# One side pair in each of eight K/Q steps, K first, with a padded hT and kv constants set ahead of the fold

## The chip, the core and the metric

The kernel runs on one core of a Trainium2 chip. A core has five engines with queues of their own: TensorE (PE, matrix products), VectorE (DVE), ScalarE (ACT, activations), GpSimd (POOL) and SyncE (SP, which issues DMAs). They meet only at semaphores. TensorE writes into eight PSUM banks of 512 float32 columns. The metric is the device time of one execution in microseconds (us), lower is better; the number for a kernel is the median of several runs.

## What is computed

The input x (2048 tokens, 448 features) is normalised (LN1) to xn. Two branches read xn and are added to x: a linear attention whose feature map is a softmax of q or k times a learned w_phi and of its negative, and an MLP mixer with a GELU layer, token shifts of 1, -1, 2 and -2 on four feature groups, a second product (W2), a second layer norm (LN2) and an MLP with W3 and W4. Cut to what matters:

```python
def A(x, wqkv, w_phi, wo):                       # 16 heads of 28
    q, k, v = heads(x @ wqkv)
    phi_q = concat([softmax(q @ w_phi), softmax(-(q @ w_phi))])
    phi_k = concat([softmax(k @ w_phi), softmax(-(k @ w_phi))])
    kv, z = phi_k.T @ v, phi_k.sum(tokens)
    return ((phi_q @ kv) / (phi_q @ z + 1e-6)) @ wo

def B(x, w1, w2, w3, w4):
    h = gelu(layernorm(x) @ w1)                  # 448 wide
    hs = concat([shift(h[:, 112*m:112*m+112], s) for m, s in enumerate((1, -1, 2, -2))]) @ w2
    x1 = x + hs
    return x1 + gelu(layernorm(x1) @ w3) @ w4    # 1792 wide inside

xn = layernorm(x)
out = x + A(xn, wqkv, w_phi, wo) + B(xn, w1, w2, w3, w4)
```

## The kernel before

Tokens are 16 tiles of 128, or 4 groups of 512. The program is written as one list of operations (class Recorder): each is appended to the queue of its engine in the order of the code, and `solve` puts a semaphore wait ahead of an operation wherever it touches a piece of memory that another engine wrote or reads. Pieces are tracked by whole PSUM banks and, in SBUF, by grains of 32 bytes of a row (and by halves of 64 partitions). Two tensors or rows that share a grain are therefore ordered even if no byte is common. A queue runs strictly in its order, so a wait holds all that stands behind it.

hT holds the GELU outputs transposed, four feature groups m in a row of the region, each HW = S + 8 = 2056 columns of two bytes, 4112 bytes: 128 and a half grains.

The stages, in order: LN1, the transposes of xn, V of the first tiles and W1 (`octet`); the fold of w_phi into wq and wk (`phi_blocks` makes a block-diagonal matrix bd in the tile g_tok by a product with a mask on VectorE; `fold` multiplies by it; VectorE casts the results to wpk and wpq); then the K/Q steps; then W3 by pairs of 128 features (`w3_pair`, its two halves are a(p) and b(p) in the last list), attention outputs (`num_tile`, N) and the last product (`fin_pair`, f), all by the order written out in `play([...])`.

A K/Q step ps (0 to 7) handles two token tiles of K in banks 2 and 3 (`k_pair`), half a token group of Q in banks 0 and 1 (`q_pair`), and, where `side` names one, a W2 pair or a V pair of two tiles in banks 4 and 5. Each pair is two halves of matmuls, k[0] and k[1] and so on, because the 448 rows of a contraction are split over 64-row halves of the array that run two at a time. Then come: two exponentials of K and two of Q on ScalarE; the kv products of two tiles from two steps earlier, which accumulate in banks 6 and 7 (`kv_tile`); `w2_out`, four VectorE additions that take W2 out of its banks into xn; `k_norm`, a sum and a reciprocal for each tile on VectorE and a product on POOL (1697 ns a tile); `w2_norm`, the LN2 statistics on VectorE, and after each fourth tile the scale (`ln_scale`) on POOL; `g_apply`, the LN2 result of one tile in g_tok on POOL, which `g_T` later transposes by a DMA on SP's queue into gT, the input of W3. In step 6 `kv_picks` clears a matrix (pick, shown as tile w) on POOL and fills it by four copies on VectorE; `kv_copy` and `kv_blocks` use it after all kv products to bring kv into place.

`late_3` sets constants: the padding of wpq and phik, zeros in kvq on POOL, and then ones in a column of kvq for each of four heads on VectorE. In the code it stands ahead of the fold, so its operations do so in the queues too.

Of the kernel before, what the change touches and what calls it, by code (L numbers as in the profile page):

```python
# [223 lines left out]
def bass_parallel_sum__linear_kernel_hedgehog__mixer_s_mlp__prompt_kernel(  # L224
    nc, A_x, A_wqkv, A_w_phi, A_wo, B_x, B_w1, B_w2, B_w3, B_w4, out,
):
    _, S, D = A_x.shape
# [3 lines left out]
    NT, NG, KC, NC, NM, FC, HP = 16, 4, 4, 4, 4, 14, 32  # L231
    CR = 112
    SHIFTS = [1, -1, 2, -2]
    HW = S + 8
    x2d, out2d = A_x[0], out[0]

    es = ExitStack()
    with es:
        R = Recorder(nc, es)
        total = [0]  # L240

        def region(name, nbytes):
            nbytes = -(-nbytes // 64) * 64
            total[0] += nbytes
            h = es.enter_context(nc.sbuf_tensor(name, [128, nbytes // 2], BF16))
            R.track(h, nbytes)
            return h

        def view(h, cols, dt=BF16, at=0):
            a = h[:, at // 2:at // 2 + cols * DTB[dt] // 2]  # L250
            return a if dt == BF16 else a.bitcast(dt)

        def new(name, cols, dt=BF16):
            return view(region(name, cols * DTB[dt]), cols, dt)
# [12 lines left out]
        xnT = view(xnT_r, KC * S).rearrange("p (c s) -> p c s", c=KC)  # L267
        hT_r = region("hT", NM * HW * 2)
        hT = view(hT_r, NM * HW).rearrange("p (m s) -> p m s", m=NM)
        phik_r = region("phik", NT * 1024 * 2)  # L270
# [21 lines left out]
        kvq = new("kvq", 8 * 64).rearrange("p (b e) -> p b e", b=8)  # L292
# [48 lines left out]
        dve, pool = "DVE", "POOL"  # L341
# [59 lines left out]
             [maskb[0:CR, :]], [maskb[0:CR, :]])  # L401

        def late_3():
            R.ew(pool, "memset", wpq.rearrange("p c (h e) -> p (c h) e", e=HP)[:, :, DH:HP], 0.0)
            R.ew(pool, "memset", phik.rearrange("p t g e -> p (t g) e")[:, :, DH:HP], 0.0)
            R.ew(pool, "memset", kvq[:, :, :], 0.0)
            for h in range(4):
                col = HP * (h % 2) + DH + 1
                R.ew(dve, "memset", kvq[HP * h:HP * h + DH, :, col:col + 1], 1.0)
# [5 lines left out]
        def lap(a):  # L415
            return bass.AP(a.tensor, a.offset, [list(a.ap[0]), [192, 2], [1, 256]])

        def halves(a):
            return a.rearrange("p (b e) -> p b e", b=2)
# [12 lines left out]
        def ln_apply(eng, dst, src, mvt, rst, i):  # L432
            m, op = (mvt[:, i, 0:1], ALU.subtract) if eng == dve else (rst[:, i, 1:2], ALU.add)
            R.ew(eng, "tensor_scalar", dst, src, m, rst[:, i, 0:1], op0=op, op1=ALU.mult)
# [73 lines left out]
        def two(b):  # L508
            return pairs[b // 2].rearrange("p (b e) -> p b e", b=2)

        def w1_parts(g, bs):
            def evac():
                for m in (0, 2):
                    R.act(hT[0:CR, m:m + 2, 2 + 512 * g:2 + 512 * g + 512], two(bs[m])[0:CR, :, :], ACT.Gelu_apprx_tanh)
            return (lambda k: banks[bs[k]][0:CR, :],
                    lambda m, kc, lo, hi: w1[lo:hi, kc, CR * m:CR * m + CR],
                    lambda m, kc, lo, hi: xnT[lo:hi, kc, 512 * g:512 * g + 512]), evac
# [20 lines left out]
        def row_pairs(first, second, start=False):  # L538
            for s, (p, q) in enumerate(zip(first, second)):
                for out, lhs, rhs in (p, q):  # L540
                    R.mm(out, lhs, rhs, start and s == 0, False)

        def lap_pair(outs, lhs, rhs):
            def side(k, rows, kcs):
                return [(outs[k], lhs(k, kc, *rows), rhs(k, kc, *rows)) for kc in kcs]
            return (lambda: row_pairs(side(0, LO, (0, 1, 2, 3)), side(1, HI, (0, 1, 2, 3)), True),
                    lambda: row_pairs(side(1, LO, (0, 1, 3)), side(0, HI, (0, 2, 3))))
# [16 lines left out]
        def w2_pair(i, b):  # L564
            def side(k, lo, hi):
                r = []
                for m in range(NM):
                    c0 = 2 + 128 * (i + k) - SHIFTS[m]
                    r.append((banks[2 * b + k][:, 0:D], hT[lo:hi, m, c0:c0 + 128], w2[lo:hi, m, :]))
                return r  # L570
            return (lambda: row_pairs(side(0, 0, 64), side(1, 64, CR), True),
                    lambda: row_pairs(side(1, 0, 64), side(0, 64, CR)))

        def w2_out(i, b):
            for k in range(2):
                a = banks[2 * b + k]
                R.ew(dve, "tensor_tensor", xn[:, i + k, 0:256], a[:, 0:256], xn[:, i + k, 0:256], op=ALU.add)
                R.ew(dve, "tensor_tensor", xn[:, i + k, 256:D], a[:, 256:D], xn[:, i + k, 320:512], op=ALU.add)
# [52 lines left out]
        def g_apply(i):  # L631
            ln_apply(pool, halves(g_tok[:, i % 4, :]), lap(xn[:, i, :]), mv2, rs2, i)
# [44 lines left out]

        def w3_pair(p):
            g, fc = divmod(2 * p, FC)
            b = p % 2  # L680
            a = lap_pair([banks[2 * b + k] for k in range(2)],
                         lambda k, kc, lo, hi: w3[lo:hi, kc, 128 * (fc + k):128 * (fc + k) + 128],
                         lambda k, kc, lo, hi: gT[lo:hi, g % 2, kc, :])

            def late():
                a[1]()
                R.act(h3T[:, g % 2, fc:fc + 2, :], two(2 * b), ACT.Gelu_apprx_tanh)
            return a[0], late
# [70 lines left out]
        v, w = v_parts(0, (4, 5, 6, 7)), w1_parts(0, (0, 1, 2, 3))  # L759
# [7 lines left out]
        v, w = v_parts(8, (4, 5, 6, 7)), w1_parts(1, (0, 1, 2, 3))  # L767
        octet(w[0], ([], [(xn_T, 10, 4)], [(xn_T, 11, 5)]), w[1], v[0], ([], [(phi_blocks, 0)]), v[1])
        a, b = w1_parts(2, (0, 1, 2, 3)), w1_parts(3, (4, 5, 6, 7))
# [6 lines left out]
        def w2_norm(i):  # L776
            for j in (i, i + 1):
                ln_stats(st2, mv2, xn, j)
            if i % 4 == 2:
                ln_scale(mv2, rs2, i - 2, 4, 4)  # L780

        wa, wb = w2_pair(0, 1), w2_pair(2, 0)
        wa[0]()
        wb[0]()
        wa[1]()
        w2_out(0, 1)
        wb[1]()
        w2_out(2, 0)
        w2_norm(0)
        w2_norm(2)  # L790
        side = {1: ("w", 4), 2: ("w", 6), 3: ("v", 12), 4: ("v", 14), 5: ("w", 8), 6: ("w", 10)}
        for ps in range(8):
            k, q = k_pair(2 * ps, 1), q_pair(ps // 2, 2 * (ps % 2), 0)
            kind, i = side.get(ps, ("", 0))
            w = {"w": w2_pair, "v": v_pair}[kind](i, 2) if kind else ()
            k[0]()
            if w:
                w[0]()
            else:
                q[0]()  # L800
            k[1]()
            for s in range(2):
                k_exp(2 * ps, 1, s)
            if ps > 1:
                kv_tile(2 * ps - 4)
                kv_tile(2 * ps - 3)
            if w:
                q[0]()
                w[1]()
            if kind == "w":  # L810
                w2_out(i, 2)
            if kind == "v":
                R.act(vaug[:, i:i + 2, :].rearrange("p t (h e) -> p t h e", e=HP)[:, :, :, 0:DH],
                      two(4)[:, :, 0:D].rearrange("p t (h e) -> p t h e", e=DH), ACT.Copy)
            q[1]()
            for s in range(2):
                q_exp(2 * ps, 0, s)
            k_norm(2 * ps)
            if kind == "w":
                w2_norm(i)  # L820
            if ps > 0:
                g_apply(ps - 1)
            if ps == 4:
                for i in range(4):
                    g_T(i)
            if ps == 6:
                kv_picks()
# [3 lines left out]
        wl = {i: w2_pair(i, 2) for i in (12, 14)}  # L831

        def a(p):
            return (w3p[p][0],)

        def b(p):
            return (w3p[p][1],)
# [4 lines left out]
        def N(i):  # L842
            return (lambda: (num_tile(i), o_T(i)),)

        def K(*t):
            return (lambda: [kv_tile(i) for i in t],)

        def w2_last(i):
            wl[i][1]()
            w2_out(i, 2)  # L850
            w2_norm(i)

        def G(*t):
            return (lambda: [g_T(i) for i in t],)
# [4 lines left out]
        def A(*t):  # L859
            return (lambda: [g_apply(i) for i in t],)  # L860

        play([
            a(0), (wl[12][0],), b(0), a(1), (w2_last, 12), b(1), A(7), K(12, 13), G(4, 5),
            a(2), (wl[14][0],), b(2), a(3), (w2_last, 14), b(3), G(6, 7), A(8, 9, 10, 11),
            K(14, 15), (kv_copy,), a(4), a(5), b(4), (kv_blocks,), b(5),
            a(6), N(0), b(6), a(7), f(1, 0), b(7), N(1), a(8), b(8), f(2, 0), G(8, 9), a(9), N(2), b(9),
            a(10), f(3, 0), b(10), f(4, 0), G(10, 11),
            a(11), N(3), b(11), f(1, 1), a(12), N(4), b(12), f(2, 1), S(0, 1),
# [49 lines left out]
```

## Time and profile before

| | us |
|---|---|
| three runs | 190.83, 192.46, 193.15 |
| median | 192.46 |
| profiled execution, time on the device | 190.65 |
| its span, first to last instruction | 188.9 |

A row of the timeline reads: start, length, engine, line of the code, operation, written tile, read tiles, shape, how many were merged, and in brackets how long the engine had been idle just before and what ended that. Lines L203, L207, L211 and L215 are the helpers that record every operation, so the tiles tell what a row is: bank<-wpk,xnT is K, bank<-xnT,wpq is Q, bank<-w,hT is W2, bank<-gT,w is W3, bank<-vaug,phik is kv, bank<-xnT,w with 112 rows is W1. On VectorE, xn<-bank,xn is the taking out of W2, ksum the norms of K, st the LN2 statistics (of xn). On ScalarE, phik<-bank of 896 elements are the exponentials of K, eq_lo and hi those of Q. Matmuls are pipelined: the length of a group runs past the start of the next, so the pace is read from start to start.

### The profile page before, as it was taken

The numbers are of one execution on the slowest core, as the hardware profiler recorded it, in microseconds if no ns is written. First come the engines' busy times: TensorE is split into PE (matmuls) and PEld (weight loads), VectorE is DVE, ScalarE is ACT, GpSimd is POOL, SyncE is SP. The second block draws the span as 40 slices with busy tenths as digits, with TensorE's granted clock in tenths as the row PEclk, the third lists the DMA queues.
The fourth block names the chain that finished last, engine by engine and source line by source line (L and its number), as shares of the span: only waits on it lengthen the run. The fifth ranks groups of instructions, "written<-read, shape, count | busy, mean of one in ns | idle before, by whom it ended". The sixth has DMA issues, their size and how long they took to land.

```text
span 188.9 us, 4746 instructions
## 1 busy us (share of the span) xinstructions
PE 174.6 (92%) x2031; PEld 97.6 (52%) x2031; DVE 113.0 (60%) x282; ACT 82.4 (44%) x92; POOL 97.2 (51%) x144
## 2 busy tenths in 40 slices
PE   7699979987999997589899999999999999999993
PEld 5345535433669975245554555454555545555451
DVE  5799636388799669666864375154642536464531
ACT  2359833708869977654463242222422224224000
POOL 5667850005679998848275226844062440732740
PEclk9999999999999999999999999999999999999999
DMA  5994259930001111110201243203532030211321
GB/s 169 371 223 87 54 100 371 348 94 0 3 9 24 28 31 28 31 28 4 55 5 28 59 70 73 76 0 80 111 59 76 3 88 20 76 31 28 79 78 48
DMA packets 32979, 14.85 MB, mean 79 GB/s; under 512 B 24703, under 2 KB 32447, under 8 KB 32959
## 3 DMA queue, kind: packets, MB, share of 16 engines
q1 hardware_dynamic: 31710, 13.58, 28.9%
q10 hardware_dynamic: 1248, 0.98, 1.6%
q8 instruction: 16, 0.26, 0.6%
q14 instruction: 5, 0.03, 0.1%
HBM read 7.08 MB, written 1.84 MB: 47 GB/s over the span
## 4 chain that ended last, share of the span: by engine, by line
PE 72%; DVE 12%; POOL 7%; ACT 4%; issue 2%; DVEq 0%
PE bank L203 72%; DVE xn L215 4%; DVE st L215 3%; POOL rs L215 3%; ACT hi L211 2%; ACT phik L211 2%; POOL xn L215 2%; DVE mv L215 1%; DVE ksum L215 1%; POOL phik L215 1%; POOL mv L215 1%; DVE vaug L215 1%; DVE w L215 1%; ACT hT L211 1%; DVE rks L215 0%
## 5 line engine op out<-in xcount | busy, mean ns | idle before, releaser
L211 ACT ACTIVATE phik<-bank 128x1024 bf16<-128x1024 f32 (+1 forms) x44 | 42.3, 984 | 70.0 <-PE bank L203 70.0
L203 PE MATMUL bank<-gT,w 64*128 64x512 bf16 x392 | 50.6, 377 | 2.6 <-ACT hi L211 2.5
L215 DVE TENSOR_TENSOR vaug<-bank,vaug 128x464 f32<-128x464 f32 (+3 forms) x65 | 32.6, 512 | 25.1 <-PE bank L203 23.5
L203 PE MATMUL bank<-w,phik 64*128 64x448 bf16 (+1 forms) x420 | 45.0, 349 | 0.1
L215 POOL TENSOR_TENSOR xnT<-vaug 128x196 bf16<-128x196 f32 (+1 forms) x32 | 18.1, 585 | 45.9 <-DVE vaug L215 45.9
L203 PEld LDWEIGHTS bank<-w,phik 64*128 64x128 bf16 (+1 forms) x420 | 21.7, 94 | 21.8 <-PE bank L203 0.5
L215 POOL TENSOR_TENSOR phik<-phik,rks 128x896 bf16<-128x896 bf16 x16 | 26.8, 1697 | 7.3 <-DVE rks L215 7.3
L203 PEld LDWEIGHTS bank<-gT,w 64*128 64x128 bf16 x392 | 18.6, 94 | 20.2 <-ACT hi L211 3.0
L215 DVE TENSOR_REDUCE ksum<-phik 128x32 f32<-128x896 bf16 x16 | 16.8, 1052 | 1.7 <-ACT phik L211 1.7
L203 PE MATMUL bank<-xnT,wpq 64*128 64x512 bf16 x112 | 16.3, 376 | 1.5 <-ACT hi L211 1.3
L215 POOL TENSOR_SCALAR mv<-mv 128x1 f32<-128x1 f32 (+2 forms) x16 | 3.6, 225 | 26.6 <-DVE mv L215 26.0
L215 DVE RECIPROCAL vaug<-bank 128x16 f32<-128x16 f32 x16 | 4.1, 257 | 21.8 <-PE bank L203 21.8
L215 POOL TENSOR_TENSOR vaug<-xn,xtok 128x448 f32<-128x448 bf16 x16 | 16.2, 1031 | 1.2 <-DVE vaug L215 1.2
L203 PE MATMUL bank<-wpk,xnT 64*128 64x448 bf16 x112 | 15.0, 349 | 1.4 <-ACT phik L211 1.2
L203 PE MATMUL bank<-w,hT 64*128 64x448 bf16 (+1 forms) x128 | 15.6, 350 | 0.4 <-ACT hT L211 0.4
L203 PE MATMUL bank<-xnT,w 128*112 128x512 bf16 (+1 forms) x64 | 14.7, 385 | 1.4 <-DVE g_tok L215 1.4
L215 DVE TENSOR_TENSOR xn<-bank,xn 128x256 bf16<-128x256 f32 (+1 forms) x32 | 10.0, 378 | 8.6 <-PE bank L203 8.6
L203 PE MATMUL bank<-wv,xnT 64*128 64x448 bf16 (+1 forms) x76 | 13.6, 352 | 0.3 <-DVE xn L215 0.2
L203 PE MATMUL bank<-wo,xnT 64*128 64x448 bf16 (+1 forms) x106 | 13.4, 349 | 0.0
L215 POOL TENSOR_SCALAR g_tok<-xn,rs 128x512 bf16<-128x512 bf16 x16 | 12.1, 767 | 0.0
L215 POOL TENSOR_TENSOR rs<-mv,mhalf 128x1 f32<-128x1 f32 (+2 forms) x16 | 11.3, 705 | 1.3
L211 ACT ACTIVATE hT<-bank 112x1024 bf16<-112x1024 f32 x8 | 7.9, 1024 | 7.7 <-PE bank L203 7.7
(67 smaller groups left out, 182.9 us busy)
## 6 DMA issues: line engine op xcount, KB each, us to landing
w<-in_B_w_dram SPq DMA_DIRECT2D x2, 896.0 KB, 5.8
out_dram<-vaug SPq DMA_DIRECT2D x15, 112.0 KB, 1.9
w<-in_B_w_dram SPq DMA_DIRECT2D x1, 1568.0 KB, 11.8
xtok<-in_A_x_dram SPq DMA_DIRECT2D x2, 448.0 KB, 6.8
xtok<-in_A_x_dram SPq DMA_DIRECT2D x2, 224.0 KB, 5.1
w<-in_B_w_dram ACTq DMA_DIRECT2D x2, 224.0 KB, 5.3
wo<-in_A_wo_dram SPq DMA_DIRECT2D x2, 224.0 KB, 6.9
w<-in_B_w_dram SPq DMA_DIRECT2D x1, 392.0 KB, 8.0
```

What stands on the lines that cost most here:

```text
L203: self.op("PE", lambda e: e.matmul(out, lhsT, rhs, start=start, stop=stop, skip_group_check=True), [out], [lhsT, rhs], tile=self._tile(lhsT))
L211: self.op("ACT", lambda e: e.activation(out, in_, func, **kw), [out], [in_] + aps)
L215: self.op(eng, lambda e: getattr(e, name)(out, *args, **kw), [out], aps)
```

## The change

Five edits. The rows of hT are padded from 2056 to 2064 columns (4128 bytes, 129 whole grains). `late_3` clears kvq first, and the ones in kvq leave it for a function `kv_ones`, called after the fold. The two W2 pairs ahead of the K/Q steps move into steps 0 and 1, and the list `side` gives each of the eight steps one W2 or V pair, so that each step runs k[0], w[0], k[1], kv, q[0], w[1], q[1]. `g_apply` runs two steps behind instead of one, and the first four `g_T` move from step 4 to step 5. The W3 pairs swap banks (the first one in 2 and 3), and the statistics of the last two W2 pairs move later in the list.

```diff
-    HW = S + 8
+    HW = S + 16
...
         def late_3():
+            R.ew(pool, "memset", kvq[:, :, :], 0.0)
             R.ew(pool, "memset", wpq.rearrange("p c (h e) -> p (c h) e", e=HP)[:, :, DH:HP], 0.0)
             R.ew(pool, "memset", phik.rearrange("p t g e -> p (t g) e")[:, :, DH:HP], 0.0)
-            R.ew(pool, "memset", kvq[:, :, :], 0.0)
+
+        def kv_ones():
             for h in range(4):
...
         def w3_pair(p):
             g, fc = divmod(2 * p, FC)
-            b = p % 2
+            b = 1 - p % 2
...
-        wa, wb = w2_pair(0, 1), w2_pair(2, 0)
-        wa[0]()
-        wb[0]()
-        wa[1]()
-        w2_out(0, 1)
-        wb[1]()
-        w2_out(2, 0)
-        w2_norm(0)
-        w2_norm(2)
-        side = {1: ("w", 4), 2: ("w", 6), 3: ("v", 12), 4: ("v", 14), 5: ("w", 8), 6: ("w", 10)}
+        kv_ones()
+        side = [("w", 0), ("w", 2), ("w", 4), ("v", 12), ("v", 14), ("w", 6), ("w", 8), ("w", 10)]
...
             k[0]()
-            if w:
-                w[0]()
-            else:
-                q[0]()
+            w[0]()
             k[1]()
...
-            if w:
-                q[0]()
-                w[1]()
+            q[0]()
+            w[1]()
...
-            if ps > 0:
-                g_apply(ps - 1)
-            if ps == 4:
+            if ps > 1:
+                g_apply(ps - 2)
+            if ps == 5:
                 for i in range(4):
                     g_T(i)
...
         def w2_last(i):
             wl[i][1]()
             w2_out(i, 2)
-            w2_norm(i)
...
-            a(0), (wl[12][0],), b(0), a(1), (w2_last, 12), b(1), A(7), K(12, 13), G(4, 5),
+            a(0), (wl[12][0],), b(0), a(1), (w2_last, 12), b(1), (w2_norm, 12), A(6, 7), K(12, 13), G(4, 5),
             a(2), (wl[14][0],), b(2), a(3), (w2_last, 14), b(3), G(6, 7), A(8, 9, 10, 11),
-            K(14, 15), (kv_copy,), a(4), a(5), b(4), (kv_blocks,), b(5),
+            K(14, 15), (kv_copy,), (w2_norm, 14), a(4), a(5), b(4), (kv_blocks,), b(5),
```

On POOL, ahead of the fold, the memset of kvq moves past those of wpq and phik:

```order
 L215 TENSOR_SCALAR xn<-xtok,rs 128x512
+L215 MEMSET kvq 128x512
 L215 MEMSET wpq 128x64x4
 L215 MEMSET phik 128x512x4
-L215 MEMSET kvq 128x512
```

It is first of the three now; the four VectorE memsets that read its result stand behind all casts of the fold.

On TensorE, from the last W1 matmuls to the second K/Q step:

```order
 L203 MATMUL bank<-g_tok,hi 128x112 x4
 L203 MATMUL bank<-xnT,w 112x512 x6
-L203 MATMUL bank<-w,hT 128x448 x32
 L203 MATMUL bank<-wpk,xnT 128x448 x8
+L203 MATMUL bank<-w,hT 128x448 x8
+L203 MATMUL bank<-wpk,xnT 128x448 x6
 L203 MATMUL bank<-xnT,wpq 128x512 x8
-L203 MATMUL bank<-wpk,xnT 128x448 x6
+L203 MATMUL bank<-w,hT 128x448 x8
 L203 MATMUL bank<-xnT,wpq 128x512 x6
 L203 MATMUL bank<-wpk,xnT 128x448 x8
```

The block of 32 W2 matmuls is gone from there; its first half stands in step 0 between the halves of K and of Q, its second half in step 1.

On VectorE, at the end of step 6 and in step 7, before:

```order
L215 BN_STATS st<-xn 128x6
L215 BN_AGGR mv<-st 128x2
L215 COPY w<-ident 32x128 x4
L215 TENSOR_REDUCE ksum<-phik 128x32
L215 RECIPROCAL rks<-ksum 128x32
```

and after:

```order
L215 BN_STATS st<-xn 128x6
L215 BN_AGGR mv<-st 128x2
L215 COPY w<-ident 32x128 x4
L215 TENSOR_TENSOR xn<-bank,xn 128x256
L215 TENSOR_TENSOR xn<-bank,xn 128x192
L215 TENSOR_TENSOR xn<-bank,xn 128x256
L215 TENSOR_TENSOR xn<-bank,xn 128x192
L215 TENSOR_REDUCE ksum<-phik 128x32
L215 RECIPROCAL rks<-ksum 128x32
```

Step 7 has a W2 pair now, and its `w2_out` stands right behind the copies that fill pick, which wait for POOL. What POOL does ahead of that memset (w), before:

```order
L215 TENSOR_TENSOR phik<-phik,rks 128x32x28 x2
L215 TENSOR_SCALAR mv<-mv 128x4
L215 TENSOR_TENSOR rs<-mv,mhalf 128x4
L215 TENSOR_SCALAR rs<-mv 128x4
L215 TENSOR_SCALAR g_tok<-xn,rs 128x512
L215 MEMSET w 128x256
```

and after:

```order
L215 TENSOR_TENSOR phik<-phik,rks 128x32x28 x2
L215 TENSOR_SCALAR g_tok<-xn,rs 128x512
L215 MEMSET w 128x256
L215 TENSOR_TENSOR phik<-phik,rks 128x32x28 x2
L215 TENSOR_SCALAR mv<-mv 128x4
L215 TENSOR_TENSOR rs<-mv,mhalf 128x4
```

The scale of four tiles that stood ahead of the memset comes a step later, behind the K norms of step 7.

More of the change, by code (lines that the diff above doesn't have):

```diff
@@ L780, in w2_norm @@
                 ln_scale(mv2, rs2, i - 2, 4, 4)
-        wa, wb = w2_pair(0, 1), w2_pair(2, 0)
-        wa[0]()
-        wb[0]()
-        wa[1]()
-        w2_out(0, 1)
-        wb[1]()
-        w2_out(2, 0)
-        w2_norm(0)
-        w2_norm(2)
-        side = {1: ("w", 4), 2: ("w", 6), 3: ("v", 12), 4: ("v", 14), 5: ("w", 8), 6: ("w", 10)}
+        kv_ones()
+        side = [("w", 0), ("w", 2), ("w", 4), ("v", 12), ("v", 14), ("w", 6), ("w", 8), ("w", 10)]
         for ps in range(8):
             k, q = k_pair(2 * ps, 1), q_pair(ps // 2, 2 * (ps % 2), 0)
-            kind, i = side.get(ps, ("", 0))
-            w = {"w": w2_pair, "v": v_pair}[kind](i, 2) if kind else ()
+            kind, i = side[ps]
+            w = {"w": w2_pair, "v": v_pair}[kind](i, 2)
             k[0]()
-            if w:
-                w[0]()
-            else:
-                q[0]()
+            w[0]()
             k[1]()
```

## Prediction, made before the changed kernel was run

> **What bounds the kernel now.** I read the page's first part, then TensorE's list of waits, then the timeline of each engine from 24 us to 95 us, then the windows by stage.
>
> ```profile
> PE 174.6 (92%) x2031; PEld 97.6 (52%) x2031; DVE 113.0 (60%) x282; ACT 82.4 (44%) x92; POOL 97.2 (51%) x144
> PE bank L203 <- ACT hi L211: 3.8, 2, 2.5
> 44.47:80.77 36.30, 32.26 (x480) 24.29 (x480) 28.99 (x60) 28.93 (x33) 30.83 (x26) 1.00 0.10 20
> ```
>
> TensorE is the bound, and the change removes none of its matmuls, so all it can win is TensorE's idle time, all of which that can move lies before 95 us. In the third row (one window: length, busy time of PE, PEld, DVE, ACT, POOL, then granted clock, DMA share, GB/s) TensorE idles 4.0 us in the K/Q steps, most of it in the two waits of the second row.
>
> The first place is the fold of w_phi, in the timeline:
>
> ```profile
> 24.22 0.39 PE L203 MATMUL bank<-g_tok,rsel 28*112 28x448 bf16 x1
> 25.48 0.52 POOL L215 MEMSET kvq<- 128x512 bf16 x1
> 26.09 0.46 DVE L215 MEMSET kvq<- 28x8 bf16 x4 [3.24 <-POOL kvq L215]
> 26.56 0.62 DVE L215 TENSOR_TENSOR g_tok<-bank,maskb 112x448 bf16<-112x448 f32 x1
> 27.24 0.85 PE L203 MATMUL bank<-xnT,w 128*112 128x512 bf16 x3 [1.39 <-DVE g_tok L215]
> ```
>
> The mask product (26.56) could have run once its matmul ended at 24.61. Four small memsets stood ahead of it in VectorE's queue and waited for POOL's memset of kvq, third of three. TensorE waited 1.39 us.
>
> The second place is the opening of W2 and the first K/Q step:
>
> ```profile
> 35.41 0.74 PE L203 MATMUL bank<-w,hT 64*128 64x448 bf16 x6
> 36.60 2.63 PE L203 MATMUL bank<-w,hT 64*128 64x448 bf16 x26 [0.44 <-ACT hT L211]
> 36.56 1.28 ACT L211 ACT_TABLE_LOAD   x1
> 39.26 0.36 PE L203 MATMUL bank<-wpk,xnT 64*128 64x448 bf16 x1
> 44.47 0.93 PE L203 MATMUL bank<-wpk,xnT 64*128 64x448 bf16 x8 [1.17 <-ACT phik L211]
> ```
>
> W2 stops for the last hT write, which it shares only a grain with. Step 0 (39.26 to 44.47) takes 5.21 us for 2.83 us of K and Q matmuls.
>
> The third place is the last step, which has no side work, and what follows it:
>
> ```profile
> 75.51 1.04 PE L203 MATMUL bank<-xnT,wpq 64*128 64x512 bf16 x8 [1.27 <-ACT hi L211]
> 80.77 1.04 PE L203 MATMUL bank<-gT,w 64*128 64x512 bf16 x8 [2.54 <-ACT hi L211]
> 81.68 0.31 POOL L215 MEMSET w<- 128x256 bf16 x1
> 82.02 0.79 DVE L215 COPY w<-ident 32x128 bf16<-32x128 bf16 x4 [3.38 <-POOL w L215]
> 94.24 0.39 PE L203 MATMUL bank<-w 64*128 64x256 bf16 x4 [0.74 <-DVE w L215]
> ```
>
> TensorE waits twice for exponentials to free banks 0 and 1, and at 94.24 for the kv sum that stands behind W2 statistics.
>
> **Prices of a step.** One W2 step of before, on TensorE, and the same on the others:
>
> ```profile
> 58.81 1.01 PE L203 MATMUL bank<-wpk,xnT 64*128 64x448 bf16 x8
> 63.44 1.01 PE L203 MATMUL bank<-wpk,xnT 64*128 64x448 bf16 x8
> 64.19 1.02 PE L203 MATMUL bank<-w,hT 64*128 64x448 bf16 x8
> 64.95 0.83 PE L203 MATMUL bank<-wpk,xnT 64*128 64x448 bf16 x6
> 65.52 0.64 PE L203 MATMUL bank<-vaug,phik 64*128 64x64 bf16 x29
> 66.09 1.02 PE L203 MATMUL bank<-xnT,wpq 64*128 64x512 bf16 x7
> 66.85 1.01 PE L203 MATMUL bank<-w,hT 64*128 64x448 bf16 x8
> 67.61 0.91 PE L203 MATMUL bank<-xnT,wpq 64*128 64x512 bf16 x6
> 68.26 1.02 PE L203 MATMUL bank<-wpk,xnT 64*128 64x448 bf16 x8
> ```
>
> ```profile
> 67.91 1.28 DVE L215 TENSOR_TENSOR xn<-bank,xn 128x256 bf16<-128x256 f32 x4 [2.15 <-PE bank L203]
> 69.11 1.07 DVE L215 TENSOR_REDUCE ksum<-phik 128x32 f32<-128x896 bf16 x1
> 71.82 0.57 DVE L215 BATCH_NORM_STATS2 st<-xn 128x6 f32<-128x448 bf16 x1
> 73.25 1.25 DVE L215 TENSOR_TENSOR xn<-bank,xn 128x256 bf16<-128x256 f32 x4
> 70.78 1.73 ACT L211 ACTIVATE phik<-bank 128x896 bf16<-128x896 f32 x2 [0.29 <-PE bank L203]
> 73.52 1.94 ACT L211 ACTIVATE hi<-bank 128x1024 bf16<-128x1024 f32 x2 [1.01 <-PE bank L203]
> 70.66 3.35 POOL L215 TENSOR_TENSOR phik<-phik,rks 128x896 bf16<-128x896 bf16 x2 [0.30 <-DVE rks L215]
> 79.41 0.20 POOL L215 TENSOR_SCALAR mv<-mv 128x4 f32<-128x4 f32 x1
> 80.97 0.77 POOL L215 TENSOR_SCALAR g_tok<-xn,rs 128x512 bf16<-128x512 bf16 x1
> gT<-g_tok SPq DMA_TRANSPOSE x16, 2.5
> ```
>
> TensorE, start to start: K first half 0.75, W2 first half 0.76, K second half 0.57, kv tiles and handover 0.47, Q 0.86, W2 second half 0.76, Q 0.65: together 4.82 us, without kv 4.35. A V step is 4.63 (58.81 to 63.44). VectorE: W2 out 1.20, K norms 2.71 (1.36 a tile), W2 statistics 1.43: 5.34 us. POOL: two K norms 3.35, one g 0.77, and a scale of four tiles 1.56 (79.41 to 80.97). ScalarE: 1.73 and 1.94. So a W2 step holds more VectorE than TensorE work, 5.34 against 4.82. Before, two W2 steps in a row were the most; now there are three at each end. That is what I follow below.
>
> **The change, part by part.** The times here are on the changed kernel's own clock.
>
> *kv constants.* With kvq's memset first and the small ones after the fold, the mask product runs at 24.7 to 25.3, and TensorE, free at 25.85 (27.24 less 1.39), does not wait: -1.39 us, and the first K matmul stands at 35.41 - 1.39 = 34.02. The small memsets (0.46) now lie in VectorE's idle time ahead of the first W2 out.
>
> *hT padding, K first.* No W2 matmul waits for hT any more. Step 0 has 4.35 us of work and ends at 38.37. ScalarE's table load ends at 36.56 + 1.28 - 1.39 = 36.45, the K exponentials 1.73 later, at 38.2, which frees banks 2 and 3 in time for the next K.
>
> *Steps 0 to 4.* W2 out of step 0 starts at 37.75, as its matmuls end. From there VectorE has no break: W2 out of step 1 at 43.1, though its matmuls end at 42.1. Banks 4 and 5 come free at 44.3, while step 2 wants them at 43.5: it waits 0.9. Its own W2 out follows at 48.45, and V in step 3 (48.4 to 53.55) waits 0.5 for it. V steps need no W2 out, so VectorE catches up there. Step 4 ends at 58.2.
>
> *Steps 5 to 7.* Step 5 ends at 63.0, W2 out at 62.4; step 6 ends at 67.85, its W2 out at 67.75 (62.4 + 5.34), which holds step 7 for 0.35. Step 7 ends at 73.0, where before it was 80.77. The w3 pairs now begin in banks 2 and 3, whose exponentials ended at 72.1, so the 2.54 us wait goes; the 1.27 went with the new order in the step.
>
> *What is late next.* After the first w3 half (73.0 to 73.9) W2 pair 12 needs banks 4 and 5 from step 7's W2 out. That stands on VectorE behind the pick copies of step 6, these behind POOL's memset of pick, and this behind the K norms of step 6 and one g. POOL: the scale from 68.4 (after the K norms of step 5, started 65.05) to 70.0, g to 70.8, K norms of step 6 to 74.15, g to 74.95, memset to 75.3. VectorE: copies 0.79 to 76.1, W2 out 1.20 to 77.3. So TensorE stands still from 73.9 to 77.35: 3.45 us, a wait that before did not exist. A bound from below is 0, if POOL gets there earlier; from above it is the memset's old place, 81.68, 6.4 us later than mine. I take 3.45 since each link has a row. The transposes of g are one step later: the fourth starts at 70.8 and takes 2.5, so 73.3, which that wait covers.
>
> *To the kv blocks.* From 80.77 to 94.24 before are 13.47 us, 12.73 without the wait of 0.74. That wait goes, since the statistics of pair 14 are now behind the kv sum. VectorE's backlog costs 0.3 at pair 14 (W2 out of 12 ends 82.7, wanted at 82.4). So the blocks start at 73.0 + 12.73 + 3.45 + 0.3 = 89.5 instead of 94.24. The rest, 94.24 to the end, is TensorE without a break; the g tiles for its next group (POOL free of scale 8 at 83.9, three g to 86.2, transposes to 89.8) are there before they are wanted at about 92.
>
> **The sum.** -1.39 in the fold, -6.38 to the end of the steps (80.77 - 73.0 - 1.39), +3.45 and +0.3 of new waits, -0.74 at the blocks: -4.7 us. The profiled execution took 190.65 (span 188.9), so 185.9; the median of the three runs, 192.46, lies 1.8 above it, so about 187.8 on the median.
>
> **Rivals.** (1) *The new wait is hidden.* If POOL reaches the memset 3.45 us sooner, the time is 184.3. For it: before, no matmul waited for these copies. Against: then nothing stood behind them, now W2 out does.
>
> (2) *The clock drops in the new wait.* The longest wait of before in that stretch, 2.54 us, left the granted clock at 1.00, and the eight matmuls after it kept their pace (1.04 us). Mine is longer. At the start, TensorE after idling:
>
> ```profile
> 1.25 3.58 PE L203 MATMUL bank<-gT 128*128 128x256 bf16 x19 [1.25 <-DVE gT L215]
> ```
>
> These 256-column passes start every 0.188 us; 448-column pairs take 0.19 (0.76 for four pairs), so 256 columns at full pace would be 0.108: nineteen lost 1.5 us. The same again gives 187.8 + 1.5 = 189.3. [...]
>
> (3) *Slower: POOL's memset of pick comes late.* All of VectorE's W2 out waits behind it, and each us later costs TensorE one. The gain is gone when it ends 4.7 us later than mine, at 80.0; at its old place, 81.68, the time is 187.8 + 6.4 = 194.2. For: POOL is full from 65 on. Against: the scale that it stood behind before (79.41) comes after it now.
>
> (4) *The kv constants don't help*, something else holds the fold at 27.24: 187.8 + 1.4 = 189.2. Against: no other row of that place ends later than 25.85.
>
> (5) *Further waits of 1 to 2 us* on the path of VectorE's three W2 steps or ScalarE's kv copies: 189 to 190.
>
> **Chances.** Forecast 0.52, (1) 0.15, (2) 0.10, (3) 0.05, (4) 0.09, (5) 0.09. Faster by over 2% (about what a measurement of this kernel can tell from no change) means below 188.6: the first rival and most of the forecast, whose runs spread by about 1 us as those of before do, together 0.58. Slower is (3) and a tail, 0.06. The rest is 0.36. The range goes from the first rival to past (4) and (5): 184.4 to 190.2.
>
> **What would show it.** No wait for g_tok at about 26; no wait for hT; step 7 ending near 73; TensorE waiting about 3.4 us for VectorE's xn ahead of the second W2 group after the steps, with POOL's memset of w near 75; kv blocks near 89.5; the granted clock at 1.00 behind the wait. The forecast is wrong if the memset of pick stands elsewhere, or if TensorE shows waits behind 90 us.

## The result, and the profile after

| | before | after |
|---|---|---|
| median of the runs taken with the result, us | 192.25 (190.83 to 193.15) | 186.52 (186.39 to 187.70) |
| profiled execution, us | 190.65 | 186.41 |
| its span, us | 188.9 | 184.6 |

The ratio is 0.9722, 95% interval 0.965 to 0.9795. Ten executions of the changed kernel were timed in all (four here, six in an experiment below); their median is 187.8, and the later six alone gave 0.9823, interval 0.9785 to 0.9862. So the first set alone says faster by over 2%, the second leaves that open, and both say faster. Where this spread of one kernel comes from is the main finding of the experiments.

TensorE's list of waits of the changed kernel (waiter, waited for, total us, times, longest):

```profile
PE bank L203 <- DVE xn L215: 3.0, 6, 1.9
PE bank L207 <- DVE xn L215: 1.5, 4, 0.7
PE bank L203 <- DVE gT L215: 1.3, 1, 1.3
PE bank L203 <- DMA gT<-g_tok: 0.6, 1, 0.6
PE bank L203 <- ACT phik L211: 0.2, 1, 0.2
```

The waits for the mask product (g_tok), for the last hT write, for the Q exponentials (hi) and for the kv sum (w) are gone. What is left in this stretch is W2 out (xn), and one transposed g tile. The same in TensorE's timeline, the first group of each of the eight steps and what follows them:

```profile
25.69 0.81 PE L203 MATMUL bank<-xnT,w 128*112 128x512 bf16 x3
...
33.82 0.93 PE L203 MATMUL bank<-wpk,xnT 64*128 64x448 bf16 x8
...
38.18 0.93 PE L203 MATMUL bank<-wpk,xnT 64*128 64x448 bf16 x8
...
42.66 0.94 PE L203 MATMUL bank<-wpk,xnT 64*128 64x448 bf16 x8
43.79 0.36 PE L203 MATMUL bank<-w,hT 64*128 64x448 bf16 x1 [0.19 <-DVE xn L215]
44.38 0.93 PE L203 MATMUL bank<-w,hT 48*128 48x448 bf16 x7 [0.23 <-DVE xn L215]
...
48.36 1.02 PE L203 MATMUL bank<-wpk,xnT 64*128 64x448 bf16 x8
...
53.47 1.01 PE L203 MATMUL bank<-wpk,xnT 64*128 64x448 bf16 x8
...
58.10 1.01 PE L203 MATMUL bank<-wpk,xnT 64*128 64x448 bf16 x8
...
62.92 1.02 PE L203 MATMUL bank<-wpk,xnT 64*128 64x448 bf16 x8
...
67.88 1.02 PE L203 MATMUL bank<-wpk,xnT 64*128 64x448 bf16 x8
...
74.05 1.04 PE L203 MATMUL bank<-gT,w 64*128 64x512 bf16 x8 [0.60 <-DMA gT<-g_tok]
77.01 0.36 PE L203 MATMUL bank<-w,hT 64*128 64x448 bf16 x1 [1.92 <-DVE xn L215]
77.61 0.93 PE L203 MATMUL bank<-w,hT 48*128 48x448 bf16 x7 [0.23 <-DVE xn L215]
78.19 1.86 PE L203 MATMUL bank<-gT,w 64*128 64x512 bf16 x14
79.70 0.92 PE L203 MATMUL bank<-w,hT 64*128 64x448 bf16 x7
...
81.11 0.73 PE L203 MATMUL bank<-vaug,phik 64*128 64x64 bf16 x29
...
89.40 0.42 PE L203 MATMUL bank<-w 64*128 64x256 bf16 x4
```

Steps begin at 33.82, 38.18, 42.66, 48.36, 53.47, 58.10, 62.92 and 67.88, and the kv blocks at 89.40 where before they began at 94.24. A wait in brackets counts only modelled idle time; the true delay is from start to start. After the first W3 half (74.05, which takes 0.86) nothing runs until 77.01, and the pace is back only at 77.61: 2.7 us. VectorE and POOL at that place:

```profile
74.42 0.77 POOL L215 TENSOR_SCALAR g_tok<-xn,rs 128x512 bf16<-128x512 bf16 x1
75.13 0.31 POOL L215 MEMSET w<- 128x256 bf16 x1
75.47 0.79 DVE L215 COPY w<-ident 32x128 bf16<-32x128 bf16 x4 [2.17 <-POOL w L215]
76.27 1.28 DVE L215 TENSOR_TENSOR xn<-bank,xn 128x256 bf16<-128x256 f32 x4
```

VectorE is idle for 2.17 us ahead of the pick copies, with W2 out queued behind them: the chain is g tile, memset, copies, W2 out, TensorE.

### The profile page after: what moved, and what is told of

Read it like the earlier page. It is cut to its first block, busy times and chain, and to the rows that moved or that the text cites. A ratio compares the mean times of both kernels' runs of the same rounds, so it can differ in the third digit from the quotient of the medians.

```text
span 184.6 us, 4750 instructions
## 1 busy us (share of the span) xinstructions
PE 174.7 (95%) x2031; PEld 99.3 (54%) x2031; DVE 112.5 (61%) x282; ACT 82.7 (45%) x92; POOL 97.4 (53%) x144
## 4 chain that ended last, share of the span: by engine, by line
PE 74%; DVE 12%; POOL 7%; DMA 3%; issue 2%; ACT 1%; ACTq 0%; DVEq 0%
PE bank L203 73%; DVE xn L215 4%; POOL phik L215 3%; DVE st L215 3%; DVE ksum L215 3%; DMA xtok<-in_A_x_dram 3%; POOL rs L215 2%; DVE mv L215 1%; DVE rks L215 1%; POOL g_tok L215 1%; POOL mv L215 1%; PE bank L207 1%; ACT phik L211 1%; ACTq L221 0%; POOL xn L215 0%
## 5 line engine op out<-in xcount | busy, mean ns | idle before, releaser
L203 PE MATMUL bank<-gT,w 64*128 64x512 bf16 x392 | 51.3, 377 | 0.9 <-DMA gT<-g_tok 0.6
L203 PE MATMUL bank<-w,hT 48*128 48x448 bf16 (+1 forms) x128 | 17.4, 350 | 2.8 <-DVE xn L215 2.8
L203 PEld LDWEIGHTS bank<-w,hT 48*128 48x128 bf16 (+1 forms) x128 | 8.4, 94 | 8.9 <-DVE xn L215 5.8
```

The costliest lines, as they stand in the source:

```text
L203: self.op("PE", lambda e: e.matmul(out, lhsT, rhs, start=start, stop=stop, skip_group_check=True), [out], [lhsT, rhs], tile=self._tile(lhsT))
```

## Experiments

All spans are of one profiled execution each; medians are of all timed executions of a kernel. "Clock" is the mean granted TensorE clock of an execution. Of the long lines of the last list (`play`) only the part that changes is shown.

**The wait after the steps: is it the pick copies?** The pick matrix is made right after the fold, where POOL and VectorE idle.

```diff
         kv_ones()
+        kv_picks()
...
-            if ps == 6:
-                kv_picks()
```

> The pick matrix is made right after the fold, while POOL and VectorE idle, and not in step 6. Theory (the wait after the steps is W2 out behind the pick copies behind POOL): W2 out of step 7 starts near 73.2 and not 76.3, TensorE's 1.9 + 0.6 us of waits at the first W2 half after the steps go, span about 184.6 - 2.5 = 182.1. Rival (W2 out or the g tiles are late anyhow): span 184 or more.

Span 181.9, median 183.63, ratio to before 0.9576 (0.9535 to 0.9618). TensorE's timeline after the steps:

```profile
74.36 1.04 PE L203 MATMUL bank<-gT,w 64*128 64x512 bf16 x8 [0.73 <-DMA gT<-g_tok]
75.22 0.94 PE L203 MATMUL bank<-w,hT 64*128 64x448 bf16 x8
75.97 1.70 PE L203 MATMUL bank<-gT,w 64*128 64x512 bf16 x14
```

The W2 half follows the W3 half without a pause, and 2.7 us are won where 2.5 were expected, as much as the whole wait. The changed kernel's new wait is that for the pick copies. The clock is at 1.00 in all four executions.

**What does such a wait cost? POOL clears pick thirteen times.**

```diff
         def kv_picks():
-            R.ew(pool, "memset", pick[:, :, :], 0.0)
+            for _ in range(13):
+                R.ew(pool, "memset", pick[:, :, :], 0.0)
```

> POOL clears pick thirteen times and not once, some 12 x 0.25 = 3.0 us more ahead of the pick copies. Theory (each us there costs TensorE one, and the clock does not react to a wait of about 5 us): TensorE waits about 4.9 us for W2 out in place of 1.9, granted clock 1.00 behind it, span 187.6. Rival (the clock drops in a wait this long): the matmuls after it run at half pace for some 3 us, span 189 or more. Rival (the wait is hidden): span within 0.5 of 184.6.

The thirteen memsets took 4.73 us, so 4.4 more than one (I had set 3.0). One for one that makes a span of 189.0. It was 191.5, median 193.07, so the rival on the clock holds. POOL, TensorE and the windows there (length, busy PE, PEld, DVE, ACT, POOL, granted clock, DMA share, GB/s):

```profile
75.62 4.73 POOL L215 MEMSET w<- 128x256 bf16 x13
81.93 2.27 PE L203 MATMUL bank<-w,hT 64*128 64x448 bf16 x8 [6.14 <-DVE xn L215]
83.62 3.56 PE L203 MATMUL bank<-gT,w 64*128 64x512 bf16 x14
```

```profile
72.00:76.00 4.00, 3.01 (x28) 1.73 (x23) 1.72 (x5) 2.97 (x5) 3.94 (x5) 1.00 0.18 33
76.00:80.00 4.00, 0.00 (x0) 0.00 (x0) 0.00 (x0) 1.24 (x1) 3.41 (x11) 0.63 0.15 33
80.00:84.00 4.00, 2.03 (x10) 0.69 (x12) 3.53 (x11) 0.00 (x0) 0.38 (x2) 0.50 0.00 0
84.00:88.00 4.00, 4.00 (x26) 1.97 (x24) 2.51 (x6) 1.02 (x1) 3.83 (x4) 0.59 0.00 0
```

The clock falls to half during the wait and stays there after it (0.63 from 76 to 80 us, 0.50 to 84, 0.59 to 88): fourteen W3 matmuls took 2.99 us from start to start (83.62 to 86.61), where the changed kernel takes 1.51 (78.19 to 79.70).

**Is it TensorE's idling that lowers the clock?** The same kernel, with work for TensorE in the wait.

```diff
+        def fill(n):
+            for _ in range(n):
+                R.mm(banks[0][:, 0:256], gT[0:64, 0, 0, 0:128], gT[0:64, 0, 0, 0:256], True, True)
...
-            a(0), (wl[12][0],), b(0), a(1),
+            a(0), (fill, 56), (wl[12][0],), b(0), a(1),
```

> As the run with thirteen memsets of pick (span 191.5, granted clock 0.973), with 56 matmuls of 256 columns into bank 0, whose results nobody reads, ahead of the first W2 half after the steps, so that TensorE works through the wait. The wait for W2 out is as long as there. Theory (TensorE's idling lowers its clock afterwards): the clock stays at 1.00, the W2 and W3 matmuls behind run at full pace, span 189.0 to 189.5. Rival (the slow pace behind the wait has another cause, such as POOL or VectorE): clock and span as without the filling, 191 or more.

Span 189.0, clock 1.00 in all ten executions, median 190.84: 2.2 us less on the median and 2.5 less span than without the useless matmuls. W2 out starts 0.46 earlier in this profile (80.72 against 81.18, since the steps ran that much sooner), so the pace is better read from the W2 half to the kv tiles: 3.92 us here (81.63 to 85.55), 6.42 there (81.93 to 88.35). Its timeline and two of its windows:

```profile
75.50 6.28 PE L203 MATMUL bank<-gT 64*128 64x256 bf16 x56 [0.62 <-ACT hi L211]
81.63 1.35 PE L203 MATMUL bank<-w,hT 64*128 64x448 bf16 x8
82.64 1.86 PE L203 MATMUL bank<-gT,w 64*128 64x512 bf16 x14
```

```profile
76.00:80.00 4.00, 4.00 (x40) 3.44 (x38) 0.09 (x1) 0.75 (x1) 3.31 (x11) 1.00 0.15 33
80.00:84.00 4.00, 3.92 (x38) 2.50 (x37) 3.91 (x11) 0.33 (x1) 0.54 (x1) 1.00 0.02 4
```

So here the wait costs its own length, and TensorE's idling in it another 2.5 us by the clock.

**How often does the changed kernel pay this?** The changed kernel again, six executions.

> The changed kernel once more, nothing edited, for how often its clock drops. Theory (TensorE's one wait of about 2.5 us is near what lowers the clock, so it depends on the execution): runs at clock 1.00 with spans of 184.6 to 184.8, and some at 0.99 with spans 1.2 to 1.7 longer; median 186.4 to 187.7. Rival (the four runs seen were typical, one in four drops): median within 0.2 of 186.5.

Median 187.94, and all six at a clock of 0.99 or 0.98, where three of the four first ones were at 1.00 (spans 184.6 to 184.8). The profiled one, span 186.1, right after its wait:

```profile
74.56 1.04 PE L203 MATMUL bank<-gT,w 64*128 64x512 bf16 x8 [0.94 <-DMA gT<-g_tok]
77.17 0.36 PE L203 MATMUL bank<-w,hT 64*128 64x448 bf16 x1 [1.57 <-DVE xn L215]
77.77 1.15 PE L203 MATMUL bank<-w,hT 48*128 48x448 bf16 x7 [0.24 <-DVE xn L215]
78.35 3.54 PE L203 MATMUL bank<-gT,w 64*128 64x512 bf16 x14
...
82.95 0.73 PE L203 MATMUL bank<-vaug,phik 64*128 64x64 bf16 x29
```

Fourteen W3 matmuls again take 2.98 us (78.35 to 81.33). From the end of the wait to the kv tiles it is 5.78 us (77.17 to 82.95) against 4.10 (77.01 to 81.11) in the execution at full clock: one drop costs 1.7 us. Both of my readings were too mild: the four first runs were not typical, and a drop is the rule in this set. The six ran on chip 12, and the record does not name the chip of the first four; but on chip 0 three of four executions dropped as well, both with the kv constants and with the padding put back (below), so the chip is not needed to explain it.

**Both kernels with their wait filled.** The changed kernel with 14 such matmuls (bank 0), and the kernel before with 22 in its 2.54 us wait (bank 4).

```diff
-            a(0), (wl[12][0],), b(0), a(1),
+            a(0), (fill, 14), (wl[12][0],), b(0), a(1),
```

> The changed kernel with 14 matmuls of 256 columns into bank 0, whose results nobody reads, inside its wait for W2 out (75.5 to 77.0). The wait is not shortened. Theory (only TensorE's idling lowers the clock): every run at clock 1.00, spans 184.6 to 184.9, no run at 185.9 or above. Rival (the drops come from elsewhere): runs at 0.99 as often as without.

```diff
-            a(0), (wl[12][0],), b(0), a(1),
+            (fill, 22), a(0), (wl[12][0],), b(0), a(1),
```

> The kernel before with 22 matmuls of 256 columns into bank 4, whose results nobody reads, inside its 2.54 us wait for the Q exponentials (78.2 to 80.7). The wait is not shortened. Theory (the runs of before near 192.2, at clock 0.99, are those in which this wait lowers the clock; those near 190.6 are those in which it does not): nearly all runs at clock 1.00, median 190.6 to 190.9, where before has 192. Rival (the drop belongs to another wait, or to no wait): median within 0.3 of 192.

No drop in any of 5 and 12 executions (clock 0.998 to 1.00); of the 17 executions of the kernel before on that chip nine were at 0.99, with times of 191.6 to 193.2, and eight at 0.998 to 1.00, with 190.5 to 191.4. Filled, before has a median of 191.11 (0.9964 of unfilled, 0.9936 to 0.9992), slightly above what I expected at full clock. So this wait is where the kernel before loses its clock. The changed kernel filled gave 187.37, only 0.6 below unfilled, with spans of 185.3 to 185.9 where I had expected 184.6 to 184.9 without a drop. In its profile the kv blocks start at 89.32, as they should, but a product of wo waits later for a transposed attention tile:

```profile
104.91 0.93 PE L203 MATMUL bank<-wo,xnT 64*128 64x448 bf16 x7 [0.69 <-DMA xnT<-xnT]
```

The changed kernel has no wait there in the other two profiles. One transfer of an attention tile took 4.3 us from issue to landing here, and 2.4 to 2.5 there; why is open.

**Which of the edits count? The kv constants put back.**

```diff
         def late_3():
-            R.ew(pool, "memset", kvq[:, :, :], 0.0)
             R.ew(pool, "memset", wpq.rearrange("p c (h e) -> p (c h) e", e=HP)[:, :, DH:HP], 0.0)
...
-        def kv_ones():
+            R.ew(pool, "memset", kvq[:, :, :], 0.0)
             for h in range(4):
...
-        kv_ones()
```

> The kv constants stand where they stood before the change (kvq's memset third on POOL, the four ones ahead of the mask product on VectorE); all else as changed. Theory: TensorE waits for the mask product again, about 1.4 us near 26, everything after it is later by that, span 184.6 + 1.4 = 186.0. Rival (later waits absorb it): the wait is there but the wait for W2 out after the steps shrinks by as much, span within 0.3 of 184.6.

```profile
27.24 0.85 PE L203 MATMUL bank<-xnT,w 128*112 128x512 bf16 x3 [1.39 <-DVE g_tok L215]
```

The wait is back to the hundredth, and the later wait for W2 out did not shrink (2.19 modelled). The profiled span, 187.6, has a clock drop in it (0.991); the one execution at clock 1.00 has 186.3, against 184.6 to 184.8 with the edit. By this one execution the edit is worth 1.5 to 1.7 us.

**The padding put back** (`HW = S + 8`).

> The rows of hT have 2056 columns again; all else as changed. Theory: the first W2 half of step 0 waits for the last hT write (33.9 + 1.0 us), about 0.4 us, VectorE's first W2 out is later by as much and all behind it follows, span 184.6 + 0.4 = 185.0. Rival (K first already stands ahead of W2, so the padding does nothing): span within 0.15 of 184.6.

```profile
34.02 0.93 PE L203 MATMUL bank<-wpk,xnT 64*128 64x448 bf16 x8
34.79 0.92 PE L203 MATMUL bank<-w,hT 64*128 64x448 bf16 x8
35.55 0.73 PE L203 MATMUL bank<-wpk,xnT 64*128 64x448 bf16 x6
```

Span 184.8, and the W2 half starts 0.77 after K and ends 0.76 later, as with the padding: no wait. The rival holds, though the span is 0.05 past its bound: the 0.2 over 184.6 lie ahead of the first W2 matmul (K starts at 34.02 and not 33.82, and at 33.98 and 33.99 in two other profiles with the padding). Only the matmul on the fourth feature group shares a grain with the last hT write, and by the time it comes, with K first, that write is done. The executions of this kernel had clocks of 1.00, 0.991, 0.991 and 0.982, so its median of 188.12 says nothing of the padding.

**The banks put back** (`b = p % 2`).

> The W3 pairs use the banks of before (the first one 0 and 1). Theory: the first W3 half then waits for the last Q exponentials, to about 75.45 instead of 74.05, but the wait for W2 out behind it (to 77.0) shrinks by the same, so the span stays within 0.3 of 184.6: the swap wins nothing as long as the pick copies are late. Rival (the swap is what removed the 2.54 us wait): span 186 to 187.

```profile
75.73 1.89 PE L203 MATMUL bank<-gT,w 64*128 64x512 bf16 x8 [2.03 <-ACT hi L211]
77.41 1.96 PE L203 MATMUL bank<-w,hT 64*128 64x448 bf16 x8
```

The first W3 half waits for the exponentials, and the W2 half behind it starts at 77.41, where it also waited till 77.0 to 77.6 with the swap: that much is as expected. But here all four executions had a drop (clock 0.990, two of them 0.982), spans 185.1 to 187.5, median 188.02. Neither expectation had that. The swap moves TensorE's waiting, not its end; what it does to the clock can't be told apart from chance, as the changed kernel itself varies as much.

The spread of W2 over the steps and the moves of `g_apply`, `g_T` and the late statistics were not put back one by one. What they are worth is read from the timeline alone.

**What is left: the g tile, then VectorE.** Ahead of this the early pick matrix stays in. First the third and fourth g tile in step 4 and their transposes too (in the last list `A(6, 7)` becomes `A(7)`):

```diff
-            if ps > 1:
-                g_apply(ps - 2)
-            if ps == 5:
+            for j in ((), (), (0,), (1,), (2, 3), (4,), (5,), (6,))[ps]:
+                g_apply(j)
+            if ps == 4:
```

> As the run with the early pick matrix (span 181.9), and the third and fourth g tile are made in step 4, the later ones a step sooner. Theory: only the wait for the transpose of the fourth g tile goes, 0.7 us, span 181.2. Rival (W2 out of step 7, ready at 74.6, holds TensorE anyway): span 181.6 or more.

Span 181.5, between the two: the wait of 0.73 is gone, but W2 out of step 7 takes 0.3 to 0.4 of it back. Median 183.30, clock 1.00 throughout. Then the statistics moved off the full steps:

```diff
-            if kind == "w":
-                w2_norm(i)
-            if ps > 1:
-                g_apply(ps - 2)
-            if ps == 5:
+            for j in {3: (0, 2), 4: (4,), 6: (6,)}.get(ps, ()):
+                w2_norm(j)
+            for j in {3: (0,), 4: (1, 2, 3), 6: (4,), 7: (5,)}.get(ps, ()):
+                g_apply(j)
+            if ps == 4:
...
-            (w2_last, 12), b(1), (w2_norm, 12), A(6, 7), K(12, 13), G(4, 5),
+            (w2_last, 12), b(1), (w2_norm, 8), (w2_norm, 10), A(6, 7), K(12, 13), G(4, 5),
...
-            K(14, 15), (kv_copy,), (w2_norm, 14), a(4), a(5), b(4), (kv_blocks,), b(5),
+            K(14, 15), (kv_copy,), a(4), a(5), b(4), (kv_blocks,), b(5),
...
+            a(6), N(0), (w2_norm, 12), b(6), a(7), f(1, 0), b(7), N(1), (w2_norm, 14), a(8),
```

> As the run with the early pick matrix (span 181.9), and the W2 statistics leave the steps where VectorE is the longer engine: pairs 0 and 2 to step 3, 4 to step 4, 6 to step 6, 8 and 10 behind the steps, 12 and 14 behind the first two attention tiles. Theory (5.34 us of VectorE work in a W2 step against 4.82 on TensorE makes the waits in steps 2, 3 and 7): these waits go (0.4 + 0.8, 0.5, 0.5 us), the wait for the fourth g tile too, W2 out of step 7 costs 0.3; span 181.9 - 2.4 = 179.5. Rival (another engine, ScalarE or POOL, holds the steps as soon as VectorE does not): span 181 or more.

All of TensorE's waits in that profile:

```profile
PE bank L203 <- DVE gT L215: 1.3, 1, 1.3
PE bank L207 <- DVE xn L215: 0.7, 3, 0.4
PE bank L203 <- ACT phik L211: 0.2, 1, 0.2
```

The first two lie in the opening. The profiled span is 180.4, in an execution whose K matmuls started 0.6 later (34.44 against 33.82); the other three have 179.5 to 179.8. The median is 181.61, ratio to before 0.949 (0.9436 to 0.9545): the fastest kernel of this study, 4.9 us under the first median of the changed one.

## Why the prediction was right

By the steps of the prediction, on the profiled execution at full clock:

- *Kv constants:* K begins at 33.82 (34.02 forecast). Putting them back brings the wait of 1.39 back. Right.
- *hT padding, K first:* step 0 has no wait. Right in the sum, but one step of the reasoning gave it to two edits: the padding does nothing here, since K first alone moves W2 past the last hT write.
- *Steps:* 38.18, 42.66, 48.36, 53.47, 58.10, 62.92 and 67.88, each within 0.2 of the forecast. VectorE's 5.34 us in a W2 step against TensorE's 4.82 makes the waits of steps 2, 3 and 7; moving the statistics takes these waits away.
- *The new wait:* forecast from 73.9 to 77.35, with POOL's memset at 75.0 and W2 out at 76.1 to 77.3; seen with the memset at 75.13, W2 out from 76.27, and the W2 half at 77.01 to 77.61. The g tile landed at 74.05, not 73.3, and the wait covered it, as said. Making pick early wins 2.7 us, and making it later by 4.4 costs those 4.4 (the filled run).
- *Kv blocks and end:* 89.40 for 89.5, span 184.6 for 184.2 (188.9 less 4.7): -4.3 for -4.7. At 90.72, behind the blocks, TensorE waits (0.25 modelled) for a ScalarE activation that ran from 89.64 to 90.66, ahead of the kv copies (90.69). From the blocks to the first product with kvq it takes 2.20 us (89.40 to 91.60) where before it took 1.74 (94.24 to 95.98), which is the 0.4 that the sum missed. Rival (5) had looked for such a loss in the kv copies, and the prediction had named a wait behind 90 us as a sign against itself; it is a small one.

What was mis-sized is the clock, rival (2), "the clock drops in the new wait". It got 0.10, because "the longest wait of before in that stretch, 2.54 us, left the granted clock at 1.00". That is one execution. In 37 others of before, timed with the experiments, the clock falls in 21, in those of the changed kernel in seven of ten, and the profiled drop costs 1.7 us, near the 1.5 that the prediction worked out from the opening. Nor did it take a longer wait, as the prediction had it: the clock fell around waits of 1.57 to 2.19 us too (last section). The 1.8 us by which the median of before lay above its profiled execution, which I carried over to the changed kernel as a constant, was for the most part such a drop. The measured median, 186.52, has none; the 187.8 on record is the profile's forecast plus about one drop, and the median of all ten executions is 187.8 too. That agreement is partly luck: the forecast at full clock was 0.5 too low (185.9 for 186.41), and the prediction held a drop for unlikely.

## What to carry to other kernels

Follow each queue of the engine that releases a bank, not only its busy share: here a one-off constant, queued ahead of a needed evacuation and behind another engine's backlog, cost more than any of the waits that remained. Constants belong where their engines idle. Here waits of TensorE of 1.57 to 2.54 us cost more than their length in most executions (the clock fell in seven of ten of the changed kernel and in 21 of 37 of before), and comparing two profiles was not enough to see that: look at the granted clock of every execution, and at how much TensorE does around a wait (the table below).

## What the runs showed of the hardware

TensorE's granted clock fell to 0.50 around waits of 1.57 to 2.19 us in three profiled executions, and not in others: the changed kernel waits 0.94 and, after one W3 half, 1.57 us modelled in the execution that dropped; 0.60 and 1.92 in one that did not. With the kv constants put back a wait of 2.19 dropped it, with the banks put back one of 2.03; filling the wait of 2.54 ended the drops of before (21 of 37 executions without, none of 12 with the filling). A mean clock of 0.991 over 186 us is 1.7 us of lost clock, so about 3.3 us at half pace, and the W2 and W3 matmuls behind the wait lost 1.7. With the wait of 6.14 us the mean was 0.973, and the clock was low during the wait as well (0.63 from 76 to 80 us).

The clock records in the traces show how long it stayed low. Each stretch at half clock around these waits is 3.41 us long (78.35 to 81.76 in the changed kernel again, 79.62 to 83.03 with the constants put back, 75.68 to 79.10 with the banks put back), and 10.24, three times that, around the wait of 6.14 (77.04 to 87.28). The records of full clock in the two profiles without a drop around the wait are whole multiples too: 180.91 us, 53 times that, in the changed kernel's first profile, and 184.32, 54 times, in that of before. They begin 4.02 and 4.03 us into the span. The four drops begin at 75.68, 77.04, 78.35 and 79.62, which lie 1.3 to 3.9 us apart, so these steps of 3.41 us lay differently in different executions. What TensorE did in the 3.41 us ahead of a drop, and in the emptiest step around the wait of the two profiles in which the clock stayed up:

| profile | stretch, us | TensorE busy, us | clock behind it |
|---|---|---|---|
| kv constants put back | 76.21 to 79.62 | 0.98 | 0.50 |
| thirteen memsets | 73.63 to 77.04 | 1.38 | 0.50 |
| banks put back | 72.27 to 75.68 | 1.43 | 0.50 |
| changed kernel again | 74.94 to 78.35 | 1.61 | 0.50 |
| before | 79.12 to 82.53 | 1.76 | 1.00 |
| changed kernel, first profile | 75.70 to 79.11 | 1.86 | 1.00 |

In the four drops TensorE was busy for 0.98 to 1.61 us of such a stretch, with one wait in it or two; with 1.76 and 1.86 us the clock stayed at 1.00. An estimate from the two profiles at full clock, with the steps begun at every position in turn: a stretch with no more than 1.61 us of work comes at about three quarters of the positions in the changed kernel and at about 70% in before; drops were seen in 7 of 10 and 21 of 37. In the profiles of the six runs without any drop (39 executions: pick early, the two built on it, the three filled waits) every stretch of 3.41 us around the wait has 2.1 us of work or more.

Useless matmuls in the wait kept the clock up in all 27 executions tried (0.998 to 1.00).
